# Attention and gated MLP on one core: an opening in a fixed order, query heads parted by DMA copies, and a planner whose clocks wait for copies

## The chip, the cores and the metric

The kernel runs on one core of a Trainium2 chip. A core has five engines that run their own instruction streams and wait for each other by semaphores: TensorE (PE, matrix products into PSUM; its weight loads are listed as PEld), VectorE (DVE), ScalarE (ACT), GpSimd (POOL), and SyncE (SP), which here only issues DMAs. The metric is the device time of one execution in microseconds. Before the change it is 735.17 us, the median of 4 runs (735.07 to 735.25).

## The reference

Inputs are bf16: x of 2048 rows by 512 columns, 32 heads of 16 columns, and a hidden width of 1792. The second layer's own input B_x is not used.

```python
def layernorm(x): return (x - mean(x)) / sqrt(var(x) + 1e-5)

q, k, v = split(layernorm(x) @ wqkv)            # 32 heads of 16
p = softmax(q @ k.T * 16 ** -0.5)               # per head, 2048 x 2048
h = x + concat(p @ v) @ wo
g, u = layernorm(h) @ w_gate, layernorm(h) @ w_up
out = h + (sigmoid(g) * u) @ w_down
```

## The kernel before

**Tiles.** Scores are computed transposed: 128 keys on the partitions, queries along the free axis. The work is counted in units of 128 x 512 scores of one head, 2048 units in all. Two or three units make a score tile. TensorE writes a tile to PSUM (L1110). ScalarE turns the tile into exponentials in SBUF (L1475). Of many tiles ScalarE leaves the last unit to VectorE, which makes an approximate exponential: a conversion to 16-bit integers (tile `J`, L1292), two shifted copies of the integers that GpSimd adds (L1313), and for some pairs an addition of two of the three copies on VectorE (L1337), after which TensorE has one product less to do. TensorE then multiplies the probabilities by the values (L1268). The value tile `Vaug` has a 17th column per head that holds one half, so the row sums come out of the same product; `Vaug2` is the same tile times a weight.

**Heads.** Four pairs of heads share 128 partitions: a 32-row block holds two heads. A query tile `QT[g]` holds the queries of every second head and zeros in the rows of the others, so a product over 32 rows gives one head. `prep_q` projects 512 queries for eight heads, scales them into `qd` (L778), and `split_q` (L327) multiplies `qd` by the two columns of a 0/1 mask to make the two query tiles.

**The order of the work.** All five engines run in the order in which the program is written. The program writes it by planning: it keeps a clock per engine (`T`), adds a guessed cost for each instruction, and at each step emits what its clocks say is ready. The table `PLAN` overrides single decisions: which product comes next, which tiles leave a unit to VectorE, which pairs get the addition. Costs are constants, for example `DMA_T` (3000 ns from an instruction to the landing of the transpose that it feeds) and 9000 ns for GpSimd's change to the integer addition.

**The opening.** Rows 0 to 511 of x are needed first. They are normalized in four blocks of 128 rows (statistics `s`, root `q`, reciprocal `r`, application `a`, transpose on TensorE `t`, copy out of PSUM `e`), projected to the first queries and keys (`p`, L401), and copied to `QT` and `KT` (L406 and L415). Until then TensorE multiplies a constant tile (`fill`, L475). A loop chooses, among the tasks that its clocks say are ready, by a rank; each takes one of seven PSUM banks and gives it back. The loop also places `halves` (L265), which writes the 17th column of `Vaug` on ScalarE, and `masks` (L269 and L271) on VectorE, which makes the head masks.

**The ramp.** The other three chunks of 512 rows are normalized by VectorE (statistics) and GpSimd (L583 to L590), transposed by TensorE (chunk 1) or by a DMA issued from SP (chunks 2 and 3, L593), and projected to keys (`early_k`, copied to `KT` at L757) and values (`prep_v`, L323 and L324) while the first score tiles run.

**The rest.** Output projection, second normalization (its transposes are DMAs, `hn`, L837), gate and up products (L847), tanh (L877), and the down product (L865) run as background work between score tiles. The last 256 rows make a tail after the last exponential.

Of the kernel before, what the change touches and what calls it, by code (L numbers as in the profile page):

```python
# [22 lines left out]
PLAN = {176: 5, 239: 2, 367: 1, 383: 1, 414: 3, 432: 9, 480: 5, 492: 1, 496: 3, 512: 4, 561: 1, 592: 3, 593: 9, 606: 3, 609: 3, 736: 5, 751: 2, 780: 2, 785: 1, 796: 1, 800: 4, 831: 1, 844: 2, 849: 3, 894: 3, 897: 9, 914: 9, 928: 3, 960: 2, 976: 3, 1025: 2, 1040: 3, 1041: 5, 1052: 2, 1072: 3, 1088: 2, 1100: 2, 1104: 5, 1105: 3, 1120: 3, 1170: 1, 1233: 3, 1280: 3, 1328: 4, 1359: 2, 1392: 3, 1440: 2, 1486: 3, 1681: 1, 1824: 5, 1840: 9, 1872: 4, 1953: 3, 1982: 1, 2001: 3, 2080: 3, 2095: 2, 2129: 3, 2161: 3, 2162: 2, 2176: 4, 2222: 1, 2239: 2, 2256: 4, 2257: 9, 2274: 4, 2287: 2, 2350: 3, 2412: 1, 2430: 2, 2465: 9, 2479: 2, 2480: 9, 2512: 2, 2556: 2, 2560: 4, 2574: 2, 2588: 2, 2592: 5, 2608: 9, 2767: 1, 2818: 3, 2833: 9, 2849: 5, 2864: 3, 2908: 1, 2972: 2, 3020: 1, 3036: 1, 3056: 1, 3072: 3, 3169: 4, 3180: 2, 3184: 4, 3217: 2, 3234: 4, 3280: 4, 3360: 2, 3537: 2, 3617: 3, 3644: 2, 3681: 9, 3744: 3, 3756: 2, 3760: 3, 3820: 2, 3905: 4, 3938: 3, 3953: 3, 4066: 4, 4080: 3, 4081: 4, 4096: 2, 4112: 2, 4124: 1, 4129: 9, 4191: 2, 4204: 1, 4207: 2, 4225: 3, 4268: 2, 4284: 1, 4288: 2, 4337: 2, 4352: 3, 4398: 3, 4510: 2, 4526: 1, 4641: 4, 4700: 2, 4734: 3, 4737: 4, 4752: 9, 4754: 2, 4784: 4, 4802: 4, 4878: 3, 4880: 4, 4910: 2, 4924: 1, 4928: 1, 4930: 4, 5022: 2, 5058: 3, 5072: 4, 5090: 3, 5121: 4, 5164: 1, 5182: 3, 5185: 3, 5200: 3, 5201: 3, 5265: 4, 5280: 3, 5294: 1, 5308: 1, 5345: 2, 5359: 1, 5360: 9, 5378: 3, 5388: 1, 5424: 1, 5471: 1, 5488: 1, 5522: 2, 5553: 3, 5566: 3, 5600: 2, 5633: 4, 5650: 9, 5696: 2, 5712: 4, 5728: 4, 5742: 2, 5756: 2, 5760: 3, 5840: 2, 5906: 1, 5938: 3, 6082: 9, 6095: 2, 6096: 2, 6108: 2, 6140: 1, 6192: 3, 6194: 9, 6268: 1, 6274: 3, 6289: 4, 6319: 1, 6337: 5, 6384: 1, 6431: 2, 6432: 4, 6463: 2, 6464: 4, 6528: 3, 6544: 3, 6592: 1, 6607: 2, 6624: 1, 6641: 2, 6656: 2, 6687: 2, 6689: 9, 6753: 9, 6799: 1, 6832: 2, 6847: 2, 6865: 1, 6929: 2, 6972: 2, 6974: 1, 7024: 1, 7040: 3, 7106: 9, 7152: 5, 7154: 9, 7244: 2, 7248: 3, 7281: 3, 7296: 2, 7312: 1, 7376: 2, 7408: 9, 7410: 2, 7468: 1, 7504: 4, 7505: 2, 7520: 3, 7535: 2, 7553: 4, 7566: 3, 7570: 4, 7585: 3, 7596: 2, 7676: 1, 7681: 5, 7695: 2, 7728: 4, 7776: 3, 7793: 2, 7839: 2, 7852: 1, 7886: 2, 8016: 2, 8033: 2, 8063: 2, 8128: 2, 8209: 4, 8257: 9, 8290: 4, 8305: 9, 8338: 4, 8382: 2, 8432: 5, 8494: 3, 8529: 5, 8591: 2, 8609: 5, 8626: 2, 8706: 3, 8721: 4, 8768: 4, 8800: 4, 8848: 2, 8849: 5, 8860: 1, 8863: 2, 8881: 3, 8882: 4, 8895: 2, 8896: 3, 8897: 2, 8910: 3, 8927: 1, 8946: 4, 8961: 4, 9006: 1, 9024: 3, 9026: 9, 9054: 3, 9073: 2, 9116: 2, 9120: 3, 9137: 4, 9153: 2, 9249: 5, 9276: 2, 9358: 2, 9376: 3, 9377: 9, 9407: 1, 9408: 1, 9426: 9, 9457: 3, 9504: 2, 9518: 3, 9520: 4, 9584: 9, 9586: 4, 9600: 2, 9678: 1, 9697: 1, 9711: 2, 9727: 2, 9728: 1, 9762: 9, 9776: 4, 9792: 4, 9841: 9, 9854: 2, 9855: 2, 9857: 9, 9872: 3, 9900: 1, 9919: 2, 9932: 1, 9964: 2, 9968: 3, 10028: 2, 10032: 2, 10044: 2, 10047: 1, 10146: 2, 10160: 5, 10172: 1, 10176: 3, 10177: 3, 10210: 4, 10273: 4, 10284: 1, 10304: 3, 10334: 1, 10364: 2, 10380: 2, 10417: 9, 10433: 4, 10464: 1, 10556: 1, 10622: 1, 10624: 4, 10626: 9, 10636: 1, 10640: 4, 10690: 3, 10702: 2, 10705: 3, 10734: 3, 10754: 4, 10801: 3, 10802: 2, 10816: 2, 10848: 9, 10912: 1, 10913: 1}  # L23
# [121 lines left out]
def kernel(  # L145
# [110 lines left out]
    for k in range(32):  # L256
        nc.gpsimd.memset(ramp[:, 0, k:k + 1], float(k))
    nc.vector.memset(ident_bf[:], 0.0)
# [5 lines left out]
    def halves():  # L264
        nc.scalar.activation(out=Vaug[:, :, :, DH:VW], in_=fill[:].rearrange("p (t h o) -> p t h o", t=NT, o=1),  # L265
                             func=ACT.Copy, scale=0.5)

    def masks():
        nc.vector.tensor_reduce(out=mask[:], in_=ident_bf[:].rearrange("p (b a d) -> p a b d", a=2, d=DH),  # L269
                                axis=AX.XY, op=ALU.max)  # L270
        nc.vector.tensor_scalar(out=maskz[:], in0=mask[:], scalar1=ZS, scalar2=None, op0=ALU.mult)  # L271

# [57 lines left out]
    psp = main.enter_context(tc.tile_pool(name="psum", bufs=1, space=PSUM))  # L330
    PS = psp.tile([P, 8, QC], FP32, name="PS")
    free_banks = [5, 7, 6, 3, 2, 1, 0]
    held_banks = {}

    def bank0(key):
        b = held_banks[key] = free_banks.pop()
        return PS[:, b, :]

    def free0(key):
        free_banks.append(held_banks.pop(key))  # L340
# [7 lines left out]
    class Task:  # L348
        def __init__(self, name, deps, opts, bank=0, frees=0):
            self.name, self.deps, self.opts, self.bank, self.frees = name, deps, opts, bank, frees  # L350
            self.end = None
            tasks[name] = self

    def fixed(name, at):
        Task(name, [], []).end = at

    V, A, E = nc.vector, nc.scalar, nc.tensor

    ACT_STATS = {(0, 1)}

    def stats_task(c, i):
        src, mv = xb[c][:, i, :], mvs[c][:, i, :]

        def on_act():
            junk = work.tile([P, D], BF16, name="junk")
            A.activation(out=junk[:], in_=src, func=ACT.Identity, scale=1.0 / D,
                         accum_out=mv[:, 0:1])
            A.activation(out=junk[:], in_=src, func=ACT.Square, scale=D ** -0.5,
                         accum_out=mv[:, 1:2])
            buf["fix", c, i] = True  # L370
        Task(("s", c, i), [("x", c, i)], [("A", 1650, on_act)] if (c, i) in ACT_STATS
             else [("D", 870, lambda: ln_stats(src, mv))])
        Task(("f", c, i), [("s", c, i)], [("D", 300, lambda: fix(c, i))] if (c, i) in ACT_STATS
             else [("N", 0, lambda: None)])
# [19 lines left out]
    def copy0(c, i, eng):  # L394
        eng(out=xnv[c][:, i], in_=buf["t", c, i])
        free0(("t", i))
# [7 lines left out]
    def keys0(half, act):  # L404
        cs = slice(half * 2 * P, (half + 1) * 2 * P)
        (A.copy if act else V.tensor_copy)(out=KT[0][:, cs], in_=buf[0][:, cs])  # L406
        if half:
            free0(0)

    def query0(half, a, act=False):  # L410
        cs = slice(half * 2 * P, (half + 1) * 2 * P)
# [5 lines left out]
        if half and a:  # L417
            free0(1)

    fixed("w0", 5000.0)  # L420
    for c in range(NQC):
        for i in range(TQ):
            fixed(("x", c, i), (3150.0 + 450 * (i // 2)) if c == 0 else 4800.0 + 2100 * c + 150 * i)
            stats_task(c, i)
    for i in range(TQ):
        Task(("q", 0, i), [("f", 0, i)], [("A", 270, lambda i=i: root(i))])
        Task(("r", 0, i), [("q", 0, i)], [("D", 200, lambda i=i: V.reciprocal(
            out=rstds[0][:, i:i + 1], in_=rstds[0][:, i:i + 1]))])
        Task(("a", 0, i), [("r", 0, i)], [("D", 340, lambda i=i: apply(0, i))])
        Task(("t", 0, i), [("a", 0, i)], [("P", 400, lambda i=i: turn0(0, i))], bank=1)  # L430
        Task(("e", 0, i), [("t", 0, i)],
             [("A", 500, lambda i=i: copy0(0, i, A.copy)),
              ("D", 440, lambda i=i: copy0(0, i, V.tensor_copy))], frees=1)
        for w in (1, 0):
            Task(("p", w, i), [("e", 0, i), "w0"], [("P", 340, lambda w=w, i=i: proj0(w, i))], bank=int(i == 0))
    Task("mask", [("s", 0, 3)], [("D", 450, masks)])
    Task("halves", [("s", 0, 1)], [("A", 640, halves)])
    for h in range(2):
        for w in (1, 0):
            deps = [("p", w, 2 * h), ("p", w, 2 * h + 1)]  # L440
            if w:
                deps = deps + ["mask"]
                Task(("qt", h), deps, [("A", 450, lambda h=h: query0(h, 0, True)),
                                       ("D", 400, lambda h=h: query0(h, 0))])
                Task(("qu", h), deps, [("D", 400, lambda h=h: query0(h, 1))], frees=h)
            else:
                Task(("kt", h), deps, [("A", 410, lambda h=h: keys0(h, True)),
                                       ("D", 400, lambda h=h: keys0(h, False))], frees=h)
# [987 lines left out]
    n = -1  # L1436
# [272 lines left out]
```

## Time and profile before

| | us |
|---|---|
| median of 4 runs | 735.17 |
| the profiled execution | 735.81 |
| its span, first to last instruction | 734.0 |
| PE busy | 704.1 |
| DVE busy | 663.8 |
| ACT busy | 703.2 |
| POOL busy | 421.8 |
| first exponential starts | 13.61 |

In lines of the profile, L12 is line 12 of the kernel. Groups and timeline lines have the form: engine, operation, output<-inputs, output<-input in partitions x elements, count, then busy time and the mean of one in ns, then idle time before them and what ended it. In the lines of the timeline the two numbers ahead of the engine are the start and the time until the last of the merged instructions ends. Neighbouring instructions of an engine overlap at their ends, so the time from one end to the next is shorter than a duration. Lines of stages show the stretch, its length, the engine's busy time with the count of instructions, TensorE's granted clock (1.00 is full), the DMA engines' busy share and GB/s. Lines of waits show who waited for whom, the total in us, how often, and the longest.

### The profile page before, as it was taken

Reading aid. Unit: us, or ns where it says so; the run is one execution under the profiler, and the core shown is the slowest. Engines: PE = TensorE matmul, PEld = TensorE weight load, DVE = VectorE, ACT = ScalarE, POOL = GpSimd, SP = SyncE. Lnnn points to the kernel's source line nnn. Section 1 sums busy time; section 2 is a strip of 40 time slices with the busy share of each in tenths; the row PEclk is TensorE's granted clock in tenths of the full one; section 3 lists DMA queues with packets and bytes.
Section 4 is the critical chain, followed back from the end, with each engine's and each line's share of the span. In section 5 each row is a group of like instructions: output and inputs, shape, how many; then the busy total and the mean of one; then the engine's idle time right before and its main releaser. Section 6 shows DMA issues by size and latency. Waiting matters only on the chain.

```text
span 734.0 us, 26369 instructions
## 1 busy us (share of the span) xinstructions
PE 704.1 (96%) x11139; PEld 337.6 (46%) x11194; DVE 663.8 (90%) x1314; ACT 703.2 (96%) x787; POOL 421.8 (57%) x727
## 2 busy tenths in 40 slices
PE   8899999888999999999999999999999999999997
PEld 3222224443555445544545455445554455445564
DVE  6989999989999999999999899999999988999952
ACT  7999999999999999999999999999999999999962
POOL 2724667675665556656546656655664656656610
PEclk9999999999999999999999999999999999999999
DMA  7200005000222013220223023201322134022250
GB/s 243 47 13 1 2 1 175 2 3 2 74 75 86 11 27 100 83 57 25 59 67 86 20 70 101 66 25 31 101 60 52 39 89 116 17 44 78 83 176 18
DMA packets 80892, 44.49 MB, mean 61 GB/s; under 512 B 15488, under 2 KB 80768, under 8 KB 80768
## 3 DMA queue, kind: packets, MB, share of 16 engines
q1 hardware_dynamic: 80480, 42.48, 20.6%
q8 instruction: 89, 1.46, 0.8%
q14 instruction: 35, 0.29, 0.1%
q10 hardware_dynamic: 288, 0.26, 0.1%
HBM read 37.75 MB, written 2.10 MB: 54 GB/s over the span
## 4 chain that ended last, share of the span: by engine, by line
PE 48%; ACT 25%; DVE 20%; issue 4%; POOL 2%; DMA 1%; POOLq 0%; DVEq 0%; ACTq 0%
ACT pt L1475 17%; PE PS L1110 16%; PE PS L1268 13%; DVE J L1292 10%; PE PS L847 8%; PE PS L865 5%; ACT xnT L1475 3%; DVE J L1337 2%; POOL J L1313 2%; ACT th L877 2%; PE PS L319 1%; PE PS L314 1%; ACT QTb L1475 1%; DVE st L274 1%; ACT xb L1475 1%
## 5 line engine op out<-in xcount | busy, mean ns | idle before, releaser
L1313 POOL INT64_ADD J<-J x658 | 403.7, 626 | 261.3 <-DVE J L1292 213.2
L1475 ACT ACTIVATE pt<-PS 128x1024 f16<-128x1024 f32 (+1 forms) x512 | 513.4, 1128 | 4.3 <-PE PS L1110 3.4
L1292 DVE TENSOR_SCALAR J<-PS 128x512 int16<-128x512 f32 x623 | 411.4, 679 | 22.5 <-PE PS L1110 16.7
L1110 PE MATMUL PS<-QT,KT 32*128 32x256 bf16 (+1 forms) x3712 | 264.3, 276 | 15.0 <-ACT pt L1475 9.3
L1268 PE MATMUL PS<-J,Vaug 128*17 128x256 f16 (+1 forms) x3218 | 226.8, 279 | 0.9 <-DVE xs L1176 0.3
L1268 PE MATMUL PS<-pt,Vaug 128*17 128x256 f16 (+1 forms) x2021 | 191.9, 279 | 0.0
L1110 PEld LDWEIGHTS <-KT 32*128 32x128 bf16 x3840 | 90.3, 92 | 204.8 <-issue 201.3
L1268 PEld LDWEIGHTS <-Vaug 128*17 128x17 bf16 x5871 | 132.0, 90 | 79.9 <-issue 74.8
L847 PE MATMUL PS<-xnT,wgu 128*128 128x256 bf16 x784 | 112.5, 274 | 1.1 <-DMA xnT<-hn 0.6
L1475 ACT ACTIVATE xnT<-PS 128x1024 f16<-128x1024 f32 (+1 forms) x88 | 96.4, 1131 | 0.0
L847 PEld LDWEIGHTS <-wgu 128*128 128x128 bf16 x784 | 64.4, 98 | 39.2 <-issue 33.5
L1337 DVE TENSOR_TENSOR J<-J 128x1024 f16<-128x1024 f16 (+1 forms) x97 | 67.9, 702 | 9.8 <-POOL J L1313 9.3
L865 PE MATMUL PS<-wd,hT 128*128 128x512 bf16 x169 | 51.0, 383 | 2.3 <-issue 2.2
L1268 PE MATMUL PS<-xnT,Vaug 128*17 128x256 f16 x360 | 51.8, 273 | 0.1
L877 ACT ACTIVATE th<-PS 128x512 f32<-128x512 f32 (+1 forms) x63 | 39.1, 620 | 8.4 <-DVE hT L860 5.0
L1475 ACT ACTIVATE QTb<-PS 128x1024 f16<-128x1024 f32 x39 | 43.2, 1108 | 0.3 <-PE PS L1110 0.3
L919 DVE SCALAR_TENSOR_TENSOR hT<-th,PS 128x512 bf16<-128x512 f32 x49 | 33.2, 678 | 2.8 <-PE PS L847 2.8
L1475 ACT ACTIVATE xb<-PS 128x1024 f16<-128x1024 f32 (+2 forms) x29 | 29.9, 1093 | 0.3 <-PE PS L1110 0.3
L1176 DVE STREAM_TRANSPOSE xs<-PS 128x256 f32<-128x256 f32 (+1 forms) x60 | 27.5, 458 | 1.8 <-PE PS L1268 1.6
L1475 ACT ACTIVATE pe<-PS 128x1024 f16<-128x1024 f32 (+2 forms) x26 | 26.0, 1061 | 1.7 <-PE PS L1110 1.6
L1268 PE MATMUL PS<-QTb,Vaug 128*17 128x256 f16 x156 | 27.1, 274 | 0.0
L1147 DVE TENSOR_TENSOR o<-xs,rsum 128x128 bf16<-128x128 f32 (+1 forms) x60 | 24.2, 404 | 2.1
(126 smaller groups left out, 395.6 us busy)
## 6 DMA issues: line engine op xcount, KB each, us to landing
wgu<-in_B_w_gate_dram SPq DMA_DIRECT2D x49, 256.0 KB, 3.0
wgu<-in_B_w_up_dram SPq DMA_DIRECT2D x49, 256.0 KB, 3.4
out_dram<-ob SPq DMA_DIRECT2D x16, 128.0 KB, 1.7
wd<-in_B_w_down_dram SPq DMA_DIRECT2D x1, 1792.0 KB, 8.7
xr<-in_A_x_dram SPq DMA_DIRECT2D x14, 128.0 KB, 3.5
xb<-in_A_x_dram SPq DMA_DIRECT2D x6, 256.0 KB, 6.2
J<-in_B_w_gate_dram SPq DMA_DIRECT2D x4, 384.0 KB, 5.6
J<-in_B_w_up_dram SPq DMA_DIRECT2D x4, 384.0 KB, 6.4
```

Of the source, the lines that this page charges most:

```text
L847: nc.tensor.matmul(ps[:, 0:PARTS[r][2]].rearrange("p (i q) -> p i q", q=P), lhsT=w[:, d, :], rhs=hn_of(r)[:, :, d, :], start=(d == 0), sto ...
L865: nc.tensor.matmul(ps, lhsT=hT[:, f, i * P:(i + 1) * P], rhs=wd[:, f, :], start=(f == 0), stop=(f == FC - 1))
L877: nc.scalar.activation(out=th[:, 0:ps.shape[-1]], in_=ps, func=ACT.Tanh, scale=0.5)
L919: nc.vector.scalar_tensor_tensor(out=hT[:, f:f + k, 0:w], in0=th[f][:].rearrange("p (k n) -> p k n", k=k), scalar=1.0, in1=ps2.rearrange(" ...
L1110: nc.tensor.matmul(pss[:, ui, i * CW[qc]:(i + 1) * CW[qc]], lhsT=KT[g // 2][32 * j:32 * j + 32, k * P:(k + 1) * P], rhs=q[32 * j:32 * j + ...
L1147: nc.vector.tensor_tensor(out=o2[:, 0:w // 32, DH * a:DH * a + DH], in0=xs[:, 0:w // 32, 0:DH], in1=rec.to_broadcast([P, w // 32, DH]), op ...
L1176: j = dve(650 - ns[0], lambda: nc.vector.transpose(out=xs[:, 0:w // 32, :].rearrange("p b r -> p (b r)"), in_=src), LAST, st["xs"], pr=-1)
L1268: nc.tensor.matmul(dst[32 * j:32 * j + VW, 0:w], lhsT=un.v[:, kt * SPAN[qc] + i, h, :], rhs=un.ap[:, i * w:(i + 1) * w], start=clears and ...
L1292: nc.vector.tensor_scalar(out=J[:, 0, k, :], in0=src, scalar1=ZOFF, scalar2=float(-min(CHORDS)), op0=ALU.add, op1=ALU.max)
L1313: nc.gpsimd.int64_add(words(s), words(0), CHORDS[s - 1] * (1 + 2 ** 16 + 2 ** 32 + 2 ** 48))
L1337: nc.vector.tensor_tensor(out=f1, in0=f1, in1=J[:, 0, 0:k, :].bitcast(FP16), op=ALU.add)
L1475: ex = nc.scalar.activation(out=pt, in_=pss[:, 0:wa, :], func=ACT.Exp, scale=AS)
```

## The change

- The opening no longer chooses at run time of the program's writing: the list `START` gives engine and task in order, with fixed PSUM banks. Costs change, and the clocks now add a delay between an engine's end and another engine's sight of it. Only block 1's statistics are on ScalarE, as before; the third and fourth projection of the keys, the second query tile and the second half of the keys come after the first score tile.
- The masks are made right after the identity matrix. The 17th column of `Vaug` is written by GpSimd in two halves. GpSimd's change of configuration for its normalization work is issued behind the mask, by a tiny instruction. The accumulator's memset moves to the start.
- The multiplications by the mask are gone from `prep_q`. Query tiles 2 to 7 are filled with zeros by six DMAs at the start and `QTb` by a memset; then each `prep_q` issues eight DMAs from SP, each copying the 16 rows of one head from `qd`.
- The planner's clocks: `scores` waits for keys and queries, `av` takes a unit only when its values are there, a transpose's landing counts 4000 ns, the eight copies 3300 ns, GpSimd's change to the integer addition 6000 ns. `PLAN` is another table.

```diff
-PLAN = {176: 5, 239: 2, ...}
+START = "As1 Ds0 Ds2 Aq0 Dr0 Da0 Pt0 Aq2 Df1 Ds3 Aq1 Ae0 Pp10 Dr2 Da2 Aq3 Aexps Dr1 Da1 Dr3 Da3 Pt2 De2 Pt1 Pp00 Pt3 Ae3 Pp12 De1 Pp01 Dkt0 Pp11 Dqt0 Pp13 Aqt1".split()
+PLAN = {64: 3, 128: 1, ...}
...
+    acc = PS[:, 0, :]
+    nc.vector.memset(acc, 0.0)
+    nc.vector.memset(QTB[:], 0.0)
+    for q in QT[2:]:
+        nc.sync.dma_start(out=q[:], in_=QTB[:, 0, :])
...
-    def halves():
-        nc.scalar.activation(out=Vaug[:, :, :, DH:VW], in_=fill[:].rearrange("p (t h o) -> p t h o", t=NT, o=1),
-                             func=ACT.Copy, scale=0.5)
+    def halves(i):
+        one = ramp[:, i, 0:1]
+        nc.vector.memset(one, 0.5)
+        t = slice(i * NT // 2, (i + 1) * NT // 2)
+        nc.gpsimd.tensor_copy(out=Vaug[:, t, :, DH:VW].rearrange("p t h o -> p t (h o)"),
+                              in_=one.rearrange("p (a o) -> p a o", a=1).to_broadcast([P, NT // 2, H]))
+    masks()
+    halves(0)
+    nc.gpsimd.tensor_scalar(out=ramp[:, 0, 1:2], in0=ramp[:, 0, 1:2], scalar1=1.0, scalar2=None, op0=ALU.mult)
...
-    free_banks = [5, 7, 6, 3, 2, 1, 0]
+    BANKS = {("t", 0): 5, ("t", 2): 7, ("t", 1): 6, ("t", 3): 1, 0: 2, 1: 3}
...
+    for word in START:
+        t, eng = tasks[word[1:]], word[0]
+        ns, fn = t.opts[eng]
+        at = max([free[eng]] + [seen(d, eng) for d in t.deps])
+        if eng == "P":
+            keep_warm(at)
+            at = max(at, free["P"])
+        t.end, t.eng = at + ns, eng
+        free[eng] = t.end
+        fn()
+    go = max([free["P"]] + [seen(n, "P") for n in ("qt0", "qt1", "kt0", "exps")])
+    keep_warm(go)
+    halves(1)
...
-    DMA_T = 3000.0
+    DMA_Q = 3300.0
+    DMA_T = 4000.0
...
-        job = pm_out(dve(603, lambda: nc.vector.tensor_scalar(
-            out=qd[:], in0=ps, scalar1=ZS, scalar2=None, op0=ALU.mult), st["mark"]))
-        done["q", qc, p] = [dve(262, lambda a=a: split_q(dst, a, qd), job) for a in range(2)]
+        def scale():
+            nc.vector.tensor_scalar(out=qd[:], in0=ps, scalar1=ZS, scalar2=None, op0=ALU.mult)
+            for k in range(2 * QC // 128):
+                rows = slice(DH * k, DH * k + DH)
+                nc.sync.dma_start(out=dst[k % 2][rows], in_=qd[rows])
+        job = pm_out(dve(603, scale, st["mark"]))
+        done["q", qc, p] = [Later(job, DMA_Q)]
...
+        T["P"] = max(T["P"], at + LAT)
         T["P"] = max(T["P"], ex_end.get(n - 2, 0.0) + LAT)
...
     def av_ready(loose):
         return [un for un in avq if un.u[:2] == gseq[st["cur"]] and un.end is not None
-                and un.end + LAT <= T["P"] + loose]
+                and un.end + LAT <= T["P"] + loose and values_in(un, loose)]
...
-            T["G"] += 9000.0
+            T["G"] += 6000.0
...
     pss_n = {0: scores(0)}
+    for i in (2, 3):
+        proj0(0, i)
+    pe_time("dense", 560.0)
+    query0(None, 1)
+    T["D"] = max(T["D"] + 660.0, T["P"] + DRAIN + LAT) + 430.0
+    keys0(1, False)
```

## The prediction

> **What bounds the kernel now.** I read the page first, then ScalarE's busy time by stage, then the timeline of the opening, then the waits.
>
> ```profile
> span 734.0 us, 26369 instructions
> PE 704.1 (96%) x11139; PEld 337.6 (46%) x11194; DVE 663.8 (90%) x1314; ACT 703.2 (96%) x787; POOL 421.8 (57%) x727
> ```
>
> Three engines are nearly full, so busy shares do not say which sets the pace. The stages do (length, then ScalarE's busy time):
>
> ```profile
> 13.61:24.00 10.39, 10.15 (x12) 1.00 0.27 84
> 24.00:34.00 10.00, 8.38 (x11) 1.00 0.34 66
> 34.00:44.00 10.00, 9.06 (x11) 1.00 0.21 42
> 520.00:640.00 120.00, 120.00 (x133) 1.00 0.23 65
> 640.00:660.00 20.00, 19.41 (x22) 1.00 0.19 37
> ```
>
> From the first exponential at 13.61 to the end of the last near 701.0, ScalarE stands still 6.5 us (summed over the twelve stages asked for), 2.6 of them between 24 and 44 us. It is the pace. Its timeline prices its work:
>
> ```profile
> 10.60 2.40 ACT L265 ACTIVATE Vaug<-fill 128x512 bf16<-128x512 bf16 x1
> 13.10 0.37 ACT L406 CAST KT<-PS 128x256 bf16<-128x256 f32 x1
> 13.61 1.94 ACT L1475 ACTIVATE pt<-PS 128x1024 f16<-128x1024 f32 x2
> 211.76 0.60 ACT L877 ACTIVATE th<-PS 128x512 f32<-128x512 f32 x1
> 212.24 7.46 ACT L1475 ACTIVATE pt<-PS 128x1024 f16<-128x1024 f32 x8
> ```
>
> Neighbours overlap: eight exponentials take 7.46 us, the first 1.04, so each further one of two units costs (7.46 - 1.04)/7 = 0.917 us (a unit is 128x512 scores). A tanh of one unit costs 212.24 - 211.76 = 0.48, so a unit more or less is 0.43. The kernel is thus 13.6 us of opening, 687.4 us of ScalarE, 33 us of tail.
>
> TensorE in the opening and the wait inside 24 to 44 us:
>
> ```profile
> 1.31 7.02 PE L475 MATMUL PS<-fill 128*128 128x512 bf16 x18 [1.31 <-POOL fill L252]
> 8.16 0.61 PE L308 MATMUL PS<-ident_bf,xn 128*128 128x128 bf16 x8
> 12.23 0.83 PE L401 MATMUL PS<-xnT,w 128*128 128x128 bf16 x12 [0.63 <-DVE QT L415]
> PE PS L1110 <- DVE KT L757: 1.1, 1, 1.1
> PE PS L847 <- DMA xnT<-hn: 0.6, 1, 0.6
> ```
>
> The fill matmuls stand before the first transpose in TensorE's order: their weight loads start at 1.71, 2.13 and so on up to 7.25, one per 0.43 us, and only then closer.
>
> **The opening: -1.2 us.** I lay the new order out with the durations of the old rows and 0.04 us from an engine's end to the next one's start (as between the ScalarE root ending at 6.88 and VectorE's reciprocal at 6.92). The mask work (0.28 + 0.17) now precedes the statistics on VectorE, so its first statistics start at 3.9 instead of 3.71 and end at 4.8. The first root still runs from 4.9 to 5.2, since ScalarE's own statistics end at 5.0. The new order normalizes block 0 at once (xn at 5.7 to 6.1) instead of collecting four reciprocals until 7.0. But 13 fills at 0.43 hold TensorE to 1.31 + 5.55 = 6.9, so the transposes end near 7.4, ScalarE's copy at 8.0 and the first projection runs at 8.2. VectorE copies block 2 at 8.9 to 9.3 and block 1 to 9.6; keys from 10.1 to 10.5; first query half to 10.9. The last projection waits for that copy, as its predecessor did at 12.23, so it runs 11.0 to 11.4; ScalarE's query half ends at 11.9, the scores at 12.35, and the first exponential starts at 12.4 instead of 13.6. The 2.4 us on L265 are gone from ScalarE; GpSimd does them in two halves, covered by its 13.8 us of idleness before 16.17. Bounds: -1.4 if the fills end sooner, -0.4 if TensorE stays at one fill per 0.43 us past 8.6, for then the four fills between transpose and projection push the latter to about 9.0 (4 x 0.43 after 7.4).
>
> [...]
>
> The memsets of the accumulator (0.49, at 14.03 before) and QTb (priced like it) fall into VectorE's 1.45 us of idleness before 2.41; left uncovered they would cost 1.0. SP gets six 128 KB copies of zeros, issued after the last load (landed 17.25) and ahead of the transposes that began at 25.9: covered. GpSimd's configuration change moves from 2.38 to behind the mask, about 4.4. The second one bounds its price: GpSimd idled 6.0 us at 36 to 42. It would end at 10.4, and is needed at about 14.5. Were it to need all the 13.8 us that hid the first one, the norms would start 3.7 us late.
>
> **ScalarE's work: -1.3 us.** In the built order ScalarE gets 648 exponentials of two units, 40 of three and 6 of one, instead of 651, 40 and 3: three units fewer, 3 x 0.43.
>
> **24 to 44 us: -1.0 us.** Keys of chunk 1 (L757) were ready at 28.84, after the score tile that needed them. VectorE's statistics of chunk 1 started at 14.42; now they start at about 12.9, and GpSimd's second pair of norms ends at 20.8 instead of 23.5. The projection stands at the same place in TensorE's order (between tiles 15 and 16), so even with the data early there remain projection 0.9, copy 0.7, scores 0.4 and gaps against two exponentials of 0.92: some 0.5 us of idleness each for chunks 1, 2 and 3. 2.6 becomes 1.6. Bounds: -2.6 (none left), +1.0.
>
> **Later waits: -0.6 us.** The clock of transposes grows from 3.0 to 4.0 us, and the one wait for hn (0.6, near 654) should go. The new plan table reorders the rest; bounds -3.9 (all ScalarE idleness gone) and +3.
>
> **Query heads by DMA: 0.** Thirty multiplications (L327) leave VectorE, 12.1 us busy by their two groups. The order gives it 14 more two-tile additions at 0.745 less one at 0.44 and 3 more conversions at 0.68: +12.0. VectorE stays as full as it was, and ScalarE is the cover. In exchange SP issues 120 copies. One issue took 0.36 to 0.51 us and a 128 KB store landed after 1.7, so eight land 7 x 0.45 + 1.7 = 4.9 us after the scaling (0.68), against 1.5 us for VectorE. A unit lasts 687.4/2048 = 0.336 us; in the built order the distance from projection to first use is 20.5 units (6.9 us) once and at least 41 (13.8 us) else. Only the one is close, behind two transposes on SP (1.3 each): 0 to +1.3. Behind the copies on SP stand gate loads and hn transposes, later by up to 3.3 us.
>
> [...] The trace shows the second gate load issued 0.05 us after the first's issue, 2.5 us before that one landed, so I take the overlapped price.
>
> **Tail: +0.5 us.** Fourteen down matmuls instead of twelve stand between the last transposes and the gate products: 2 x 0.30 (51.0 us/169). Bounds 0 and 1.
>
> Sum: -1.2 - 1.3 - 1.0 - 0.6 + 0 + 0.5 = -3.6. The profiled execution took 735.8 (span 734.0), 0.6 above the median of 735.17; so 732.2 against itself and 731.5 against the median, rounded down by the range's wider lower end.
>
> **Rivals.**
> 1. The ramp gives the opening back: chunk keys, not ScalarE, set 24 to 44 us, and idleness there grows by what the start gained. For it: the 1.1 us wait on KT. Against: its chain starts at VectorE's statistics, which move too. Then -1.3 - 0.6 + 0.5 = -1.4: 733.8. Chance 0.14.
> 2. Slower: SP's bursts hold hn transposes beyond the 4.0 us that the plan reckons, TensorE waits in order, ScalarE starves. One collision costs up to 3.3 us; in the built order one burst stands directly before a transpose. From two it decides: -3.6 + 6.6, 738.2. Against: only one such wait before. Chance 0.08.
> 3. The plan fits far better and takes most later idleness: 729.3. For: the waits it now counts are those seen at 28.9 and 654. Against: the order still has projection and use adjacent. Chance 0.16.
> The likeliest has 0.62.
>
> The range 728.8 to 734.9 holds rivals 1 and 3 with the opening's and plan's bounds, and leaves out rival 2. A run differs measurably from no change beyond about 0.2% (1.5 us): faster 0.80, same 0.12, slower 0.08.
>
> **What would show it.** First exponential at 12.0 to 12.9; ScalarE idle 24 to 44 below 2; 694 exponentials; no wait of TensorE on QT copies above 1.3 us; last exponential about 697. I am wrong if ScalarE's idleness after 60 us (3.5) grows, if the fills hold the transposes past 8, or if TensorE waits for DMAs.

## The result, and the profile after

The changed kernel takes 737.93 us, the median of 38 runs (731.66 to 747.34), against 735.11 before (58 runs, 734.51 to 735.75): a ratio of 1.0029, interval 1.0016 to 1.0042. I had forecast 731.5. The comparison leaves out executions more than 1.5% above the kernel's fastest, so the ratio, if anything, flatters the change.

The median hides what happened. The kernel before repeats within 1.3 us in these 58 runs; the changed one is spread over 16 us, in steps. With all its executions (the later ones of this study included) sorted by TensorE's mean granted clock:

| mean clock | executions | time, us |
|---|---|---|
| 0.999 or 1.0 | 13 | 731.37 to 732.53 |
| 0.997 | 1 | 733.20 |
| 0.993 | 10 | 736.23 to 738.07 |
| 0.991 | 13 | 737.78 to 741.05 |
| 0.989 | 2 | 738.97 to 740.37 |
| 0.984 | 5 | 742.14 to 743.30 |
| 0.982 | 3 | 743.16 to 744.75 |
| 0.979 | 2 | 745.54 to 747.34 |

The kernel before showed 0.998 to 1.0 in all executions listed beside these runs. A straight line through the 49 points gives 6.95 us for each 0.01 of clock lost. Three of the 49 were profiled, at 731.48, 731.37 and 733.20 us; none of the 35 at a clock of 0.993 or less was.

The profile that came with the result is of an execution at the full clock (731.48 us). It looks almost as forecast. First the head of its page, then ScalarE by stage (stretch, length, busy time with count, clock, DMA share, GB/s):

```profile
span 729.7 us, 26496 instructions
PE 702.7 (96%) x11111; PEld 336.0 (46%) x11169; DVE 664.9 (91%) x1301; ACT 699.7 (96%) x785; POOL 429.5 (59%) x730
```

```profile
12.04:24.00 11.96, 10.61 (x12) 1.00 0.56 180
24.00:34.00 10.00, 10.00 (x12) 1.00 0.33 66
34.00:44.00 10.00, 8.99 (x10) 1.00 0.21 41
44.00:60.00 16.00, 15.06 (x17) 1.00 0.04 10
...
500.00:660.00 160.00, 159.43 (x178) 1.00 0.24 66
660.00:697.60 37.60, 37.56 (x45) 1.00 0.36 102
```

The first exponential starts at 12.04 instead of 13.61, the last ends at 697.56 instead of 700.97, and from 24 to 44 us ScalarE stands still for 1.0 us instead of 2.6. New is a loss of 1.35 us before 24 us, against 0.24 in the kernel before. GpSimd's and TensorE's timelines of the same execution show where it comes from (start, time to the end of the last merged instruction, then the work; in brackets the idle time before it and its cause):

```profile
15.23 0.26 POOL L287 TENSOR_SCALAR ramp<-ramp 128x1 bf16<-128x1 bf16 x1 [10.00 <-issue]
15.46 1.34 POOL L282 COPY Vaug<-ramp 128x256 bf16<-128x256 bf16 x1
16.88 0.24 POOL L539 TENSOR_SCALAR nv<-mv 128x2 f32<-128x2 f32 x1
...
18.34 1.56 POOL L546 TENSOR_SCALAR xn<-xb,mv,rstd 128x512 bf16<-128x512 bf16 x2
```

```profile
17.96 0.39 PE L1068 MATMUL PS<-QT,KT 32*128 32x512 bf16 x2
19.18 0.40 PE L694 MATMUL PS<-ident_bf,xn 128*128 128x128 bf16 x4 [0.83 <-POOL xn L546]
19.96 0.40 PE L694 MATMUL PS<-ident_bf,xn 128*128 128x128 bf16 x4 [0.39 <-POOL xn L546]
```

GpSimd's configuration change was issued at 4.95 us (L287's tiny instruction carries it). GpSimd runs nothing until 15.23, 10.3 us later, and then the second half of the constants, 1.34 us, still stands ahead of chunk 1's norms. These start at 16.88 although their statistics were ready at 14.62. TensorE, working in order, reaches chunk 1's transposes at 18.34 and waits twice, 0.83 and 0.39 us. In this execution that costs little. The experiments ask whether it is also what makes the other executions long.

### The profile page after: what moved, and what is told of

Its sections match the earlier page's. It is cut to its first block, busy times and chain, and to the rows that moved or that the text cites. A ratio compares the mean times of both kernels' runs of the same rounds, so it can differ in the third digit from the quotient of the medians.

```text
span 729.7 us, 26496 instructions
## 1 busy us (share of the span) xinstructions
PE 702.7 (96%) x11111; PEld 336.0 (46%) x11169; DVE 664.9 (91%) x1301; ACT 699.7 (96%) x785; POOL 429.5 (59%) x730
## 4 chain that ended last, share of the span: by engine, by line
PE 59%; ACT 23%; DVE 9%; issue 5%; POOL 2%; DMA 1%; SPq 0%; DVEq 0%; POOLq 0%; ACTq 0%
PE PS L1068 20%; PE PS L1236 17%; ACT pt L1449 17%; PE PS L804 10%; DVE J L1260 5%; PE PS L822 5%; PE PS L330 3%; ACT xnT L1449 3%; PE PS L335 1%; ACT QTb L1449 1%; ACT xb L1449 1%; PE PS L747 1%; ACT th L834 1%; DVE J L1305 1%; PE PS L1643 1%
## 5 line engine op out<-in xcount | busy, mean ns | idle before, releaser
L1281 POOL INT64_ADD J<-J x658 | 408.2, 633 | 253.3 <-DVE J L1260 209.4
L1449 ACT ACTIVATE pt<-PS 128x1024 f16<-128x1024 f32 (+2 forms) x523 | 520.1, 1118 | 4.4 <-PE PS L1068 3.1
L1236 PE MATMUL PS<-pt,Vaug 128*17 128x256 f16 (+1 forms) x2042 | 198.2, 279 | 0.0
L1449 ACT ACTIVATE xnT<-PS 128x1024 f16<-128x1024 f32 (+1 forms) x85 | 92.3, 1119 | 0.4 <-PE PS L1068 0.2
L1305 DVE TENSOR_TENSOR J<-J 128x1024 f16<-128x1024 f16 (+1 forms) x110 | 78.5, 713 | 12.5 <-POOL J L1281 11.9
L1236 PE MATMUL PS<-xnT,Vaug 128*17 128x256 f16 x346 | 46.7, 274 | 0.0
L1449 ACT ACTIVATE xb<-PS 128x1024 f16<-128x1024 f32 (+1 forms) x25 | 26.0, 1084 | 0.3 <-issue 0.2
L1449 ACT ACTIVATE pe<-PS 128x1024 f16<-128x1024 f32 (+1 forms) x21 | 21.8, 1093 | 0.9 <-PE PS L1068 0.8
```

Of the source, the lines that this page charges most:

```text
L1236: nc.tensor.matmul(dst[32 * j:32 * j + VW, 0:w], lhsT=un.v[:, kt * SPAN[qc] + i, h, :], rhs=un.ap[:, i * w:(i + 1) * w], start=clears and ...
L1281: nc.gpsimd.int64_add(words(s), words(0), CHORDS[s - 1] * (1 + 2 ** 16 + 2 ** 32 + 2 ** 48))
L1305: nc.vector.tensor_tensor(out=f1, in0=f1, in1=J[:, 0, 0:k, :].bitcast(FP16), op=ALU.add)
L1449: ex = nc.scalar.activation(out=pt, in_=pss[:, 0:wa, :], func=ACT.Exp, scale=AS)
```

## The experiments

My theory (the dip): TensorE's idleness near 19 us makes its clock fall back to half, for some time, in most executions. Rivals: the idleness lies elsewhere, where the new plan put it; the copies of the query heads delay work at random. Times are medians, with their range.

**1. The changed kernel again.** Two more profiles, no edit.

> The changed kernel once more, for a profile of one of its longer executions; the profile at hand (731.48 us) is one of the shorter, and the runs lie at 731.7 to 747.3 us, the longer the lower the mean granted clock of TensorE (0.999 down to 0.979). Theory (the dip): TensorE is too idle between 16.5 and 20 us, where GpSimd's configuration change, and the constants queued behind it, hold chunk 1's norms; in most executions the clock falls back to half there and stays there for a number of windows. A longer execution then shows the granted clock below 1.0 in the stretch from 17 to 40 us at the latest, and 1.0 before and after. Rival (the plan): the new fillers leave TensorE too idle somewhere in 44 to 60 or 100 to 200 us; the clock falls there. Rival (the copies): the clock is 1.0 throughout and a longer execution shows waits for the query heads' transfers of over 1.3 us. Time 736 to 742 us in the median of its runs under each.

> The changed kernel once more, for one profile. Theory (the dip): with a chance of about 3 in 4 it is a throttled execution, 736 to 747 us, and then the granted clock is 0.5 from some point between 17 and 24 us, for 3 to 9 windows of 3.4 us in one piece, and 1.0 elsewhere to the last matmuls. A rival (the plan) would have the half clock somewhere behind 44 us.

The first profile met an execution at the full clock: 731.37 us, with the change over at 14.08 us, earlier than in any other profile of a kernel with the late change, and no wait of TensorE above 0.12 us at the transposes; that is the same time as the profile above, with its 1.2 us of waits. So the wait itself costs no more than the 1.2 us by which executions at the full clock differ anyway. (All eight runs of it: 738.36, 731.37 to 744.75.) The second profile met a throttled one (its clock fell), 733.20 us, milder than I had expected: one step of clock, not three to nine. TensorE by stage, cut at the times of the trace's clock records (full from 7.25, half from 20.90, full from 24.31):

```profile
14.08:17.49 3.41, 3.41 (x20) 1.00 1.09 348
17.49:20.90 3.41, 1.92 (x16) 1.00 0.35 109
20.90:24.31 3.41, 3.41 (x12) 0.50 0.00 0
```

and its timeline around the fall:

```profile
18.22 0.39 PE L1068 MATMUL PS<-QT,KT 32*128 32x512 bf16 x2
19.71 0.40 PE L694 MATMUL PS<-ident_bf,xn 128*128 128x128 bf16 x4 [1.10 <-POOL xn L546]
20.50 0.40 PE L694 MATMUL PS<-ident_bf,xn 128*128 128x128 bf16 x4 [0.39 <-POOL xn L546]
20.83 0.58 PE L1068 MATMUL PS<-QT,KT 32*128 32x512 bf16 x2
21.34 1.03 PE L335 MATMUL PS<-wv_sb,xnT 128*128 128x512 bf16 x2
```

Two value matmuls (L335) take 1.03 us there and 0.60 before. The fall comes where the theory put it, right behind the two waits, and nowhere else before the end. The clock moved in steps of 3.41 us here: 7.25 to 20.90 is four of them, 20.90 to 24.31 one. By an estimate from these times the table above is this ladder: a step at half clock is 0.5 x 3.41/730 = 0.0023 of mean clock, so 0.993 is three steps, 0.991 four, 0.979 nine, and by the slope each costs 1.6 us. That the longer executions lose their steps at the same place is concluded from the ladder and from the experiments below; no profile of the unedited kernel is of an execution above 733.20 us.

**2. The configuration change back where it was.**

```diff
+    nc.gpsimd.tensor_scalar(out=power[:], in0=power[:], scalar1=1.0, scalar2=None, op0=ALU.mult)
     ramp = prep.tile([P, 2, 32], BF16, name="ramp")
...
     halves(0)
-    nc.gpsimd.tensor_scalar(out=ramp[:, 0, 1:2], in0=ramp[:, 0, 1:2], scalar1=1.0, scalar2=None, op0=ALU.mult)
```

> GpSimd's configuration change goes back to where the ramp ends, at 2.4 us, with both constant fills (1.27 and 1.34 us) behind it. If the change is a duration, 10.3 us as it showed in the changed kernel, it ends at 12.7, the fills at 15.3, and chunk 1's first norm starts at 15.4 instead of 16.88; the dip theory then expects nearly all runs at 731 to 732 us and a clock of 0.999. If the change ends when something else does, at 15.2 to 16.2 us as it did in both kernels whether issued at 2.4 or at 4.95, the fills end at 17.9 to 18.9 and the first norm is 1 to 2 us later than in the changed kernel; the dip theory then expects more throttled runs, a median of 740 us or more. Rivals (the plan, the copies): the runs spread as those of the changed kernel, median 737 to 738 us, in both cases.

> The kernel with the early configuration change once more, for more executions: five in five at 730.2 to 730.9 us say little about a rare throttled one. Theory (the dip): the first norm waits for statistics at 14.7 us, with 1.1 us in hand behind the constant fills, so all executions again take 730.0 to 731.5 us at a clock of 0.999. If the change's length, which was 8.6 to 11.5 us in seven profiles, sometimes eats what is in hand, one or two executions lie above 733 us with a clock below 0.997.

730.34 us (five runs, 730.18 to 730.90), ratio to before 0.9937 (0.9924 to 0.9950); again 730.98 (five runs, 730.38 to 731.85), ratio 0.9944 (0.9930 to 0.9957). The clock is 0.998 to 1.0 in all ten; one of them, 731.85, lies above the 731.5 that I had allowed. GpSimd's timeline:

```profile
10.97 0.25 POOL L260 TENSOR_SCALAR power<-power 128x2 f32<-128x2 f32 x1 [8.60 <-issue]
11.19 2.36 POOL L283 COPY Vaug<-ramp 128x256 bf16<-128x256 bf16 x2
14.70 0.23 POOL L539 TENSOR_SCALAR nv<-mv 128x2 f32<-128x2 f32 x1 [1.14 <-DVE mv L293]
```

Issued at 2.4 us, the change is over at 10.97 (10.75 the second time). Both constant fills fit behind it, and the norms now wait for their statistics, as the bracket says. One line of code, moved, takes the whole spread away and beats both kernels.

**3. The second constant half behind chunk 1's norms.** The change stays late.

```diff
     keep_warm(go)
-    halves(1)
...
+        elif i == TQ - 1:          # in pool_apply, chunk 1's last block
+            halves(1)
```

> Only the second half of the constants moves behind chunk 1's last norm, so the first norm can start as soon as the configuration change is over: at 15.6 us instead of 16.88. The dip theory expects TensorE's idle time of 0.83 and 0.39 us at 18.3 to 20 us to go, ScalarE's stall of 1.36 us at 20.7 to shrink below 0.4, most runs at 730.5 to 732 us with a clock of 0.998 or more, and a median near 731.5. Rivals (the plan, the copies): chunk 1 is earlier all the same, but the spread and the median stay at 736 to 738 us, at most 1.3 us lower.

731.91 us (12 runs, 731.15 to 743.58): nine of the twelve at 0.999 or 1.0, three between 738.28 and 743.58 at 0.991 to 0.982. I expected the waits of TensorE to go altogether; in the profiled execution the change was over only at 15.72, and from 18.31 to 21.73 TensorE was still idle for 0.36 us. Taking 1.3 us off the delay makes throttling rarer, 3 in 12 instead of 36 in 49. It does not end it; the likely reason is that the length of the change itself varies, but none of the three throttled executions was profiled.

**4. Fill matmuls in the gap.** GpSimd stays as late as it was.

```diff
+                for _ in range(5 if i == 0 else 0):   # ahead of chunk 1's first transposes
+                    E.matmul(ps, lhsT=fill[:, 0:P], rhs=fill[:], start=True, stop=True)
```

> Five fill matmuls of 512 columns (0.21 us each at the full clock) are put ahead of chunk 1's first transposes, where TensorE is idle for 0.83 us; GpSimd and its change stay as they are. The dip theory expects the first norm at 16.9 us and ScalarE's stall of about 1.4 us at 20.7 still there, or up to 0.3 us longer, and still most runs at 731.5 to 732.5 us with a clock of 0.999, as the activity of TensorE between 16.5 and 20 us goes from about 0.4 to over 0.5. Rivals (the plan, the copies): nothing changes, median 737 to 738 us.

732.20 us (five runs, 731.81 to 732.73), clock 0.999 or 1.0 in all five. In the profiled execution the change was over at 16.50, later than in any other profile, the first norm started at 18.07, and ScalarE lost 2.06 us between 20 and 24 us. TensorE in the two clock steps there, and its timeline:

```profile
16.16:19.57 3.41, 3.37 (x19) 1.00 0.72 228
19.57:22.99 3.42, 2.19 (x18) 1.00 0.00 0
```

```profile
18.28 1.25 PE L693 MATMUL PS<-fill 128*128 128x512 bf16 x5
20.44 0.40 PE L696 MATMUL PS<-ident_bf,xn 128*128 128x128 bf16 x4 [0.91 <-POOL xn L546]
21.20 0.40 PE L696 MATMUL PS<-ident_bf,xn 128*128 128x128 bf16 x4 [0.36 <-POOL xn L546]
```

This run tells the theory from the rivals best: nothing is earlier, plan and copies are untouched, and useless work on TensorE brings 5.7 us. It is the idleness, not the lateness, that costs: ScalarE's stall there, 2.48 us in one piece from 19.48 us, is twice the 1.25 us of the profile that came with the result.

**5. A longer dip.** Three copies of the second constant half in place of one. In the first version VectorE's small fill ahead of each copy was repeated too.

```diff
-    halves(1)
+    for _ in range(3):
+        halves(1)
```

> The changed kernel with the second constant fill written three times instead of once, so that 2.6 us more of GpSimd's work stands ahead of chunk 1's first norm; nothing else changes. The configuration change was over at 14.1, 15.2, 15.7 and 16.5 us in four profiles, so the first norm starts at 18.1 to 20.5 us. Theory (the dip in TensorE's activity lets its clock fall): now all or nearly all runs are throttled, clock 0.993 or below, median 738 us or more, and the profile shows a granted clock below 1.0 that begins between 18 and 30 us. If instead only the stall itself costs time, the runs agree within 1.5 us at 733 to 735 us (the stall of 2.06 us in the kernel with five fills stood beside a median of 732.2).

745.84 us (six runs, 744.25 to 750.19), clock 0.975 to 0.984. It did more than I meant: the second small fill waited on VectorE for GpSimd's late copy, held all evacuations, and left TensorE idle from 14.5 to 20 us. So I repeated the copies alone:

```diff
-        nc.gpsimd.tensor_copy(out=Vaug[:, t, :, DH:VW]...)
+        for _ in range(times):     # 3 for the second half
+            nc.gpsimd.tensor_copy(out=Vaug[:, t, :, DH:VW]...)
```

> The deep dip again without what spoiled it: only the copy of the second constant half is repeated (three times instead of once), not VectorE's small fill ahead of it, which in the first version stood waiting on VectorE behind GpSimd's change and held all evacuations until 17 us. GpSimd's configuration change should end at 14 to 16.5 us, the first norm start at 17.9 to 20.4. Theory (the dip): TensorE works until about 18.3 us, then idles for 1 to 3.5 us; nearly all runs are throttled (clock 0.993 or below, 737 us or more), and the half clock of the profile begins between 18 and 25 us. If a stall costs only itself: all runs at 732 to 735 us and a clock of 0.998 or more.

744.95 us (four runs, 739.12 to 749.04), clock 0.979 to 0.992, all throttled. TensorE by clock step:

```profile
17.06:20.48 3.42, 1.34 (x7) 1.00 0.43 135
20.48:23.89 3.41, 1.49 (x10) 0.50 0.00 0
23.89:27.30 3.41, 3.41 (x14) 0.50 0.00 0
27.30:30.72 3.42, 3.42 (x20) 0.50 0.20 41
```

In this execution the half clock lasted to 47.78 us, eight steps. With more delay on GpSimd the median clock is lower, 0.982 against 0.991 in the changed kernel; the ranges overlap.

**6. The dip in the kernel before.** Opening, plan, query heads and constants of before; only the first normalization of chunk 1 is written four times.

```diff
+        for _ in range(4 if (c, i) == (1, 0) else 1):
             nc.gpsimd.tensor_scalar(out=xn[:], in0=xb[c][:, i, :], scalar1=mvs[c][:, i, 0:1],
                                     scalar2=rstds[c][:, i:i + 1], op0=ALU.add, op1=ALU.mult)
```

> The kernel before, with chunk 1's first normalization written four times on GpSimd instead of once (3 x 0.77 us): its second normalized block, and the transposes that need it, come 2.3 us later. Opening, plan, query heads and constants are those of before. Theory (the dip alone suffices): TensorE idles about 1.5 us near 20 us, and a part of the runs, perhaps most, shows a clock of 0.993 or below and 739 to 748 us, where the kernel before has none. Rival (the throttling needs the new plan or the copies): clock 0.998 or more in all runs, 735 to 737.5 us.

738.61 us (five runs, 736.78 to 739.48), ratio 1.0040 (1.0027 to 1.0053). The clock was 0.999, 0.998, 0.997, 0.994 and 0.994, so two executions were throttled by two steps and one by a single one. Most of the 3.2 us of longer time (735.37 before, beside these runs) is the delay itself: the two executions at 0.999 and 0.998 already take 736.78 and 738.15. I had expected up to 748. The profiled one:

```profile
18.50:21.91 3.41, 1.75 (x14) 1.00 0.00 0
21.91:25.32 3.41, 3.41 (x27) 0.50 0.00 0
25.32:28.73 3.41, 3.08 (x18) 0.50 0.18 37
```

The dip alone is enough to make the clock fall; neither the plan nor the copies are needed. Why it throttles more mildly here is open.

**7. The query heads.** First the two multiplications put back into the version of experiment 2, with all other work in the same order; then the copies alone put into the kernel before.

```diff
-            for k in range(2 * QC // 128):
-                rows = slice(DH * k, DH * k + DH)
-                nc.sync.dma_start(out=dst[k % 2][rows], in_=qd[rows])
+            for k in range(2):
+                split_q(dst, k, qd)
```

> The kernel with the early configuration change (730.3 us), and in it the query heads parted on VectorE as before: each scaled tile is followed by two multiplications there instead of eight copies issued by SP. The order of all other work stays. VectorE gets some 30 multiplications, about 12 us, SP loses about 120 issues. My prediction put the parting at 0, with bounds of 0 to +1.3 for the copies: then this one takes 729.0 to 730.6 us. If VectorE is closer to setting the pace than I thought, it takes up to 733 us. The clock stays at 0.999.

> The kernel before with one part of the change alone: the query heads are parted by copies on SP instead of two multiplications on VectorE (with QTB cleared at the start, and six copies of zeros). The plan, the opening and the constants stay. VectorE loses 30 multiplications, about 12 us of busy time, and the plan does not spend them. My prediction said 0, with bounds of 0 and +1.3: 735.1 to 736.5 us. From the run that put the multiplications back into the new order (+8.4 us) the other theory says that VectorE's work sets the pace as much as ScalarE's: then this one takes 727 to 732 us.

Put back: 738.79 us (738.29 to 739.75), 8.4 more than 730.34 and 7.8 more than the repeat's 730.98, all at a clock of 0.999 or 1.0, and beyond both ranges I had given. Copies alone in the kernel before: 732.56 (732.04 to 732.86), ratio 0.9965 (0.9951 to 0.9978), 2.6 less than before, between the two ranges. ScalarE by stage, with the multiplications put back:

```profile
60.00:160.00 100.00, 98.58 (x106) 1.00 0.12 33
160.00:330.00 170.00, 167.95 (x184) 1.00 0.20 55
330.00:500.00 170.00, 167.78 (x184) 1.00 0.21 56
500.00:660.00 160.00, 158.53 (x175) 1.00 0.21 61
```

From 60 to 660 us ScalarE stands still for 7.2 us, against 2.4 in the version with copies. Most of VectorE's extra work there is one group (two more multiplications, 0.6 us, write `QTb`):

```profile
L343 DVE TENSOR_SCALAR QT<-qd,mask 128x512 bf16<-128x512 bf16 x28 | 11.3, 447 | 0.5
```

So 12 us of busy time on VectorE are worth 8.4 us in this order, though VectorE's share of busy time is only 92%. In the kernel before, taking them away saves only 2.6 us; its order was not planned to use the room, which is the likely reason.

**8. Early change and late second half together.**

> The version with the early configuration change (730.3 us) and the second half of the constants behind chunk 1's last norm as well: one constant fill (1.3 us) less ahead of the norms, so that a late end of the change can hold them by less. Theory (the dip): clock 0.999 in all runs and 730.0 to 731.0 us, no faster than the early change alone in the median, since chunk 1's statistics (ready at 14.6 us) already set the first norm there. If the fill's 1.3 us ahead of chunk 2's norms at 22 us cost ScalarE time, up to 731.6.

731.30 us (five runs, 730.59 to 732.02), clock 0.998 to 1.0: not faster than the early change alone, as expected, and 0.3 above the 730.0 to 731.0 that I gave for it. The version to keep is that of experiment 2.

## Why the prediction was wrong

The sum came out near and the time was wrong: 731.5 forecast, 731.37 to 732.53 (median 732.13) in the 13 executions at the full clock, and a median of 737.93 because 36 of 49 are not at the full clock. The missing term is the clock. That the sum came out is partly luck: 2.0 us of idleness that it had not counted, before 24 us and from 44 to 60, stand against a tail 1.4 us and later waits 0.9 us better than forecast.

- **The failed step** is "GpSimd's configuration change moves from 2.38 to behind the mask, about 4.4. [...] It would end at 10.4." I took 6.0 us from the second change in the kernel before, the idle time ahead of this row:

```profile
42.00 1.94 POOL L1313 INT64_ADD J<-J x4 [5.96 <-DVE Vaug L324]
```

  The change in the opening took 9.1 to 11.5 us in seven profiles and ended at 14.1 to 16.5. My other bound, 13.8, was the better one; I kept it as a remark on norms 3.7 us late, out of the range and out of the rivals.
- **The second half of that failure** is that I priced lateness only as a stall. The stall was cheap: 731.37 without it, 731.48 with 1.2 us of TensorE's waits. The price comes from the clock that falls behind it, and the prediction has no term for that. The four runs of before agree within 0.18 us, and that kernel has no such dip: no window of its profile is below 0.50 by the measure of the last section. The clock's step was 3.41 us (13.65 us, from 7.25 to 20.90, is four of them), and full clock began anywhere from 4.66 to 7.33 us in the profiles compared under the opening. The waits ahead of the fall in the second profile of experiment 1 were 1.10 and 0.39 us.
- **Opening, -1.2:** right. The two profiles differ by 1.57 us, 13.61 to 12.04, but TensorE came to the full clock at 7.33 us in the one and at 5.90 in the other. With the full clock from 7.33 and 7.25 us (before; the second profile of experiment 1) it is 13.61 to 12.30, -1.31; with the full clock from 4.84 and 4.66 (experiment 6, whose opening is that of before; experiment 3) it is 13.19 to 12.04, -1.15. So in these profiles an earlier full clock goes with an earlier first exponential, by 0.3 to 0.4 us:

```profile
12.30 2.86 ACT L1449 ACTIVATE pt<-PS 128x1024 f16<-128x1024 f32 x3 [0.50 <-PE PS L1068]
```

- **ScalarE's units, -1.3:** 694 exponentials, as said (523 + 85 + 40 + 25 + 21 in five groups).
- **24 to 44 us, -1.0:** 1.0 us of idleness instead of the forecast 1.6, but 1.35 instead of 0.24 before 24 us, and 0.94 instead of 0.04 between 44 and 60.
- **Later waits, -0.6:** from 60 to 660 us ScalarE's idleness went from 3.7 to 2.1 us, so -1.5, not -0.6. The wait for hn is gone.
- **Query heads, 0:** right as a net term for this change, wrong as a reason. I said that ScalarE was the cover and that VectorE's time was worth nothing. In the new order 12 us of it are worth about 8. The change spends it again, on 13 more additions (110 instead of 97) and 3 more conversions (626 instead of 623). The copies cost little: TensorE's weight load and matmul waited for them at one place of note, near 273 us, and ScalarE stood still for 0.29 us behind it (0.75 in experiment 2). The copies of 16 KB, issued by SP, landed in a median of 1.8 us.

```profile
PEld L1068 <- DMA QT<-qd: 0.8, 1, 0.8
PE PS L1068 <- DMA QT<-qd: 0.5, 1, 0.5
```

- **Tail, +0.5:** wrong in sign; from the last exponential to the end 33.1 us became 32.1.
- **The range:** its upper end was the wider one (3.4 against 2.7 us), not the lower, as I wrote.
- **The rivals** do not cover the case. Number 2 had the right sign by another road, and did not happen. My list of what would show the prediction wrong held no line for a granted clock below 1, and in the profile that came with the result all lines of the list held but one: TensorE did wait for DMAs, the 0.8 us above. One profile could not have told.

## What to carry to other kernels

When a change moves anything ahead of TensorE's work, look not only at how long TensorE will wait but at the granted clock behind the wait: here waits of 1.10 and 0.39 us stood right ahead of a fall, and the 35 executions at a clock of 0.993 or less have a median of 738.91 us, 6.8 above the 732.13 of those at the full clock. Look at the spread of the times and the mean granted clock of every run before reading a profile, since one profiled execution may be one of the few good ones. Price a configuration change of GpSimd where it will run, by a row from the same stage (here 10.3 us in the opening, 5.6 at 35.9), and issue it as early as anything allows (issued at 2.4 us it was over at 10.97, issued at 4.95 at 14.1 to 16.5); and where two engines are nearly full, cost the work taken from one by an experiment in the order that will use it.

## What the runs showed of the hardware

- In the second profile of experiment 1 the clock was full for 13.65 us, four times 3.41, and then half for 3.41; in the profiles of both kernels it was full for 723.63 us, 212 times 3.413. I cut 14 profiled executions into windows of this length from the moment at which the clock became full, up to 715 us, and summed the time in which TensorE streamed columns (0.42 us per 1000, from the fills' spacing of 0.215 us per 512; matmuls side by side count once). By this count four windows stayed at or below 0.36 of their length (0.25, 0.25, 0.34, 0.36; they start at 13.35 and 17.06 us in the two versions of experiment 5, at 18.50 in experiment 6 and at 17.49 in the second profile of experiment 1), and behind each of the four the clock fell. No other window at the full clock had less than 0.44, and behind none of them did it fall. Whether TensorE's transposes count is open: left out of the sum, the same four stand at 0.25 or less and all others at 0.32 or more. The busy time of the profile's rows is a coarser measure: behind the 1.92 us of 3.41 in the second profile of experiment 1 the clock fell, and behind 1.93 us in a window of experiment 6 at 8.25 us (0.44 streamed) it did not.
- How the windows lie on the dip differed between executions: full clock began at 5.90 us in the profile that came with the result and at 7.25 in the second of experiment 1. In the first of these they cut the dip in two (0.50 and 0.57 streamed):

```profile
16.13:19.54 3.41, 2.58 (x18) 1.00 0.66 207
19.54:22.96 3.42, 2.88 (x22) 1.00 0.00 0
```

  That may be how one kernel is throttled in one execution and not in the next. It is not the whole account: by an estimate from their rows, a window of 3.41 us shifted over the three profiles of the changed kernel falls below 0.40, between the two groups, in none, a quarter and a half of its positions, and 36 of 49 executions were throttled. The long executions had a deeper dip, or something more adds; no profile shows which. Neither do the windows say why an execution loses one step or nine.
- How it comes back is open. One window at half clock with TensorE busy throughout ended it in experiment 1; in experiment 5 six windows just as full, from 23.89 to 44.37, passed before it ended at 47.78. Busy time alone does not tell these two apart, and no run tried another measure.
- GpSimd's configuration change took 8.3 to 8.6 us issued at 2.4 us, 9.1 to 11.5 issued at 4.95, and 5.6 at 35.9 in the changed kernel. In the opening the DMA engines' share was about 1.1 from 7 to 18 us, and 0.2 from 34 to 44. That the change waits for those loads fits, but was only argued: no run held the loads back. Nor did any take out the six copies of zeros, which SP issues from 10.7 us on, behind the loads; they keep the DMA engines busy longer (a share of 0.56 from 12 to 24 us, 0.38 before), and the early change was over soon after SP had begun to issue them (10.97 and 10.75 us in experiment 2).
